# Values of six token-tile pairs in Strassen form in the key/value stage of a linear-attention and SwiGLU kernel, with the x sums for the FFN kept on chip

## The chip, the cores and the metric

The kernel runs on one core of a Trainium2 chip. The metric is the device time of one execution in microseconds (us). A time of the whole kernel is the median of several runs; the trace and the profile come from one execution that was recorded. The engines are named as the profile names them: PE (matrix products; PEld is its weight loading), DVE (vector engine), ACT (scalar engine), POOL (GpSimd) and SP (which issues most DMA transfers). Each runs its own instructions in the order in which they were laid down, and waits on the others by semaphores.

## The reference, cut to what matters

S = 2048 tokens, D = 576, 32 heads of 18, F = 4608, all float32.

```python
qkv = split_heads(x @ wqkv)
pq, pk = q @ w_phi, k @ w_phi                       # per head
phi_q = concat(softmax(pq), softmax(-pq))
phi_k = concat(softmax(pk), softmax(-pk))
kv = einsum("bhsf,bhsd->bhfd", phi_k, v)            # summed over the tokens
z = einsum("bhsf->bhf", phi_k)
o = (phi_q @ kv) / (phi_q . z + 1e-6)
s = merge_heads(o) @ wo

xn = layernorm(x);  attention runs on xn
g = silu((silu(xn @ w_gate) * (xn @ w_up)) @ w_down)
return x + s * g
```

## The kernel before

**Number format.** A float32 value is held as two parts that PE multiplies at its faster float32r rate: a rounded high part (H, hi) and the rest, the low part (L, lo). A product x·w is hi·hi + hi·lo + lo·hi. D = 576 is cut into two halves of 288 (HALF), and each half of the contraction into two full chunks of 128 rows and a tail of 32 rows; for the tail the high and low parts lie on different partitions of one tile, so that a single matmul of 96 rows does all three products. So `xw` (L82) takes 14 matmuls for a 288-column product of a token tile: 2 halves of the contraction, with 3 + 3 + 1 each.

**Stages.** (1) Preparation, to 70.8 us: layernorm of the token blocks, transposes, and splitting of x into `X` (list `XB`) and of the weights into `KVWH`/`KVWL` (K weights folded with w_phi, then V weights). (2) The key/value stage, 70.8 to 227.6 us: 16 token tiles of 128. For each, K in two halves (28 matmuls into the PSUM tile `p2`, of which there is one buffer), its softmaxes (`softmax_parts`, L268 to L282: on DVE maximum, subtraction, minimum, subtraction, on ACT two exponentials, on DVE sum and reciprocal, then the product of L356 that gives `phi`), V in two halves (14 matmuls each into a tile `p`, copied by ACT to `v`, L364 to L369), and `kv_step` (L286: ten float32 products of phi with v, 20 records, accumulated over all tiles in the three PSUM tiles `kvp`). The `kv_step` of a tile is issued in the middle of the next one. (3) A transition: the column of ones in v has given z, which ten small copies bring to `zc`; matmuls with `ident` spread it over the partitions (L391), ACT copies it to `zb` (L394); the kv blocks are masked to `km` (L398) and split to KVH and KVL. (4) The Q stage (to about 470 us): Q projections, softmaxes, and attention output. (5) The FFN, already in Strassen form, to the end.

**Work beside the stages.** Some FFN tiles are computed early, in plain form, by `early_tile` (14 matmuls of 512 columns into PSUM tiles `pe`, silu on ACT, product on DVE). A scheduler lays the instructions out on the engines, and pe matmuls go where the main order leaves PE free. `spread_out` (L325) makes the x sums that the Strassen FFN reads: for each of eight token stacks k a load of the float32 tail of x into `sraw` (`load_stack`), additions of hi and lo (`raw_x`), four sums (`sums`), and `sum_parts`, which casts the sums to `shi` on ACT (L319), subtracts the tails on DVE (L320) and the rest on POOL (L321), and stores both to `sum_dram`. It has two `sraw` buffers and is stepped four times for each token tile. Stack k has two token tiles of one sequence half, four tiles apart; with the two halves of the contraction these make the four x blocks of a stack, a 2 by 2 blocking of x.

**Memory.** The tiles of these stages come from pools on two sides of SBUF; a new tile waits until earlier users of its place are done.

## Time and profile before

| | us |
|---|---|
| three runs | 1646.59, 1646.65, 1647.71 |
| median | 1646.65 |
| the execution that was profiled | 1646.79 |
| its span | 1645.0 |
| PE busy in the span | 1611.2 |
| preparation | 0 to 70.8 |
| key/value stage | 70.8 to 227.6 |
| transition | 227.6 to 238.2 |
| Q stage | 238.2 to about 470 |
| FFN | about 470 to 1645 |

How to read the rows that follow. A row of the timeline has the start in us, the duration, the engine, the line of the kernel, the operation, the tile written and the tiles read, the shape, and how many such instructions it groups (x20); in brackets stands the idle time of the engine just before it and what ended that idle time. A matmul's shape is rows of the contraction * columns of the stationary operand, then the output's columns. A row of the groups (by line, engine and shape) has busy us and the mean ns of one, then idle time before it by what ended it. A row of DMA issues has the transfer, the queue, the count, the size and the median us from issue to landing.

### The profile page before, as it was taken

To read this page: it belongs to the slowest core of one execution; us is meant where nothing else is said; L and a number is where in the kernel's file an instruction comes from. 1 tells how busy PE (TensorE), PEld (TensorE's weight loads), DVE (VectorE), ACT (ScalarE), POOL (GpSimd) and SP (SyncE) were. 2 spreads that over 40 slices of the span, in tenths; PEclk is the share of its full clock that TensorE was granted. 3 is DMA by queue.
4 is the path that set the end of the run, shared out by engine and by line. 5 is a ranking of instruction groups with operands and counts; after the bars stand their busy time and mean duration, and the time that the engine had idled before them with its cause. 6 is when DMAs were issued, how large, how long until landed. Compare 5 with 4: busy or idle time off the path is not lost.

```text
span 1645.0 us, 25213 instructions
## 1 busy us (share of the span) xinstructions
PE 1611.2 (98%) x9441; PEld 1435.0 (87%) x9441; DVE 1177.0 (72%) x1722; ACT 715.3 (43%) x1389; POOL 619.4 (38%) x660
## 2 busy tenths in 40 slices
PE   6999999999999999999999999999999999999998
PEld 5899998999987788888888888888888888888887
DVE  7678759899852476887887778845566677666578
ACT  5533345444431365444444444445433333333334
POOL 3466500343202353653554454412333244133132
PEclk9999999999999999999999999999999999999999
DMA  9623313343218545555455545495545556555434
GB/s 290 212 78 109 110 34 112 92 143 110 74 45 293 202 169 180 173 175 177 175 172 171 183 166 176 130 364 164 164 127 161 170 173 211 161 179 183 140 114 173
DMA packets 118108, 264.69 MB, mean 161 GB/s; under 512 B 12418, under 2 KB 48386, under 8 KB 116194
## 3 DMA queue, kind: packets, MB, share of 16 engines
q1 hardware_dynamic: 107628, 247.44, 45.7%
q0 software_dynamic: 3072, 11.02, 2.4%
q10 hardware_dynamic: 7286, 4.63, 0.9%
q8 instruction: 74, 1.21, 0.3%
q14 instruction: 48, 0.39, 0.1%
HBM read 164.21 MB, written 98.83 MB: 160 GB/s over the span
## 4 chain that ended last, share of the span: by engine, by line
PE 66%; DVE 1%; DMA 0%; issue 0%; ACT 0%; POOL 0%; SPq 0%; ACTq 0%; POOLq 0%; DVEq 0%
PE pd L669 24%; PE px L570 23%; PE pw L570 11%; PE py L570 6%; PE pe L92 2%; DVE acc L641 0%; DMA hb<-h_dram 0%; DVE w L59 0%; DMA X<-s_dram 0%; DVE hh L59 0%; ACT w L58 0%; DVE acc L642 0%; ACT s L599 0%; POOL ld L560 0%; DVE s L604 0%
## 5 line engine op out<-in xcount | busy, mean ns | idle before, releaser
L669 PEld LDWEIGHTS pd<-dw,hh 128*128 128x128 f32 x3048 | 431.8, 188 | 23.0 <-ACT pd L690 1.5
L669 PE MATMUL pd<-dw,hh 128*128 128x288 f32 x3048 | 447.4, 297 | 1.7 <-ACT pd L690 0.7
L570 PE MATMUL px<-X,w 128*128 128x512 f32 x1440 | 373.2, 393 | 4.6 <-ACT s L599 3.6
L570 PEld LDWEIGHTS px<-X,w 128*128 128x128 f32 x1440 | 261.3, 188 | 55.9 <-ACT s L599 6.9
L570 PE MATMUL pw<-X,w 128*128 128x512 f32 x720 | 185.5, 393 | 0.0
L570 PEld LDWEIGHTS pw<-X,w 128*128 128x128 f32 x720 | 134.8, 189 | 30.1
L92 PE MATMUL pe<-X,wh 128*128 128x512 f32 (+1 forms) x480 | 152.0, 400 | 1.9 <-DVE h L120 0.9
L604 DVE TENSOR_TENSOR s<-pw,s 128x512 f32<-128x512 f32 x120 | 82.5, 688 | 99.1 <-ACT s L599 88.3
L794 DVE TENSOR_TENSOR acc<-pd,acc 128x576 f32<-128x576 f32 x128 | 96.2, 752 | 79.4 <-PE pd L669 79.3
L599 ACT COPY s<-px 128x512 f32<-128x512 f32 x120 | 70.4, 586 | 154.7 <-PE px L570 154.7
L58 ACT CAST hh<-ha 128x512 fp32r<-128x512 f32 x140 | 82.7, 619 | 96.2 <-PE pd L669 71.0
L92 PE MATMUL p<-KVWH,X 128*128 128x288 f32 (+1 forms) x640 | 123.6, 298 | 0.7 <-DVE phi L274 0.7
L59 DVE TENSOR_TENSOR hh<-ha,hh 128x512 fp32r<-128x512 f32 x140 | 110.6, 815 | 17.6 <-ACT hh L58 15.9
L766 POOL TENSOR_TENSOR hb<-hb 128x512 f32<-128x512 f32 x34 | 45.8, 1346 | 163.8 <-DVE hb L626 163.3
L92 PEld LDWEIGHTS pe<-X,wh 128*128 128x128 f32 (+1 forms) x480 | 88.5, 189 | 19.9 <-DVE h L120 1.7
L92 PEld LDWEIGHTS p<-KVWH,X 128*128 128x128 f32 (+1 forms) x640 | 100.5, 188 | 1.4 <-issue 1.1
L59 DVE TENSOR_TENSOR w<-ld,w 128x512 fp32r<-128x512 f32 (+1 forms) x90 | 76.6, 852 | 33.2 <-ACT w L58 32.1
L570 PE MATMUL px<-X,wt 96*128 96x512 f32 x240 | 94.8, 395 | 0.0
L570 PE MATMUL py<-X,w 128*128 128x512 f32 x360 | 93.7, 395 | 0.1
L779 POOL TENSOR_TENSOR ha<-ha 128x512 f32<-128x512 f32 x34 | 52.6, 1562 | 107.2 <-DVE hh L59 107.2
L58 ACT CAST w<-ld 128x512 fp32r<-128x512 f32 (+1 forms) x90 | 49.4, 549 | 86.6 <-POOL ld L560 54.3
L753 POOL TENSOR_TENSOR h<-ha,hb 128x512 f32<-128x512 f32 x34 | 44.9, 1320 | 103.3 <-DVE ha L630 66.6
(181 smaller groups left out, 3046.5 us busy)
## 6 DMA issues: line engine op xcount, KB each, us to landing
w_dram<-w SPq DMA_DIRECT2D x87, 512.0 KB, 2.8
w<-w_dram SPq DMA_DIRECT2D x87, 512.0 KB, 4.4
wt<-t_dram SPq DMA_DIRECT2D x59, 336.0 KB, 3.4
ld<-in_B_w_gu SPq DMA_DIRECT2D x30, 512.0 KB, 4.5
X<-sum_dram SPq DMA_DIRECT2D x8, 1280.0 KB, 7.0
rt<-in_B_w_down SPq DMA_DIRECT2D x33, 288.0 KB, 3.4
rb<-in_B_w_down SPq DMA_DIRECT2D x33, 288.0 KB, 4.5
w_dram<-w SPq DMA_DIRECT2D x29, 256.0 KB
```

What stands on the lines that cost most here:

```text
L58: nc.scalar.copy(hi, src)
L59: nc.vector.tensor_sub(lo, src, hi)
L92: nc.tensor.matmul(ps, l, r, start=n == 0, stop=n == len(pairs) - 1)
L570: nc.tensor.matmul(ps, l, r, start=first and n == 0, stop=last and n == len(mm) - 1, skip_group_check=True)
L599: nc.scalar.copy(t, ps)
L604: nc.vector.tensor_add(t, ps, t)
L669: nc.tensor.matmul(ps, l, r, start=first and n == 0 and m == 0, stop=n == len(hs) - 1 and m == 2, skip_group_check=True)
L753: sub(s, g["h"][0][0], g["h"][0][1])
L766: nc.gpsimd.tensor_add(a21, a21, g["h"][1][1])
L779: sub(a12, a12, g["h"][0][0])
L794: nc.vector.tensor_add(a2, pd[:, :, 0:HALF], a2)
```

## The change

Pairs p = 2 to 7 of token tiles (stack k = (p + 4) mod 8; a pair is the two token tiles of a stack that share its weights) compute their values as a 2 by 2 by 2 Strassen product: seven products of 288 by 288 instead of eight. Four of its x operands are the blocks of x, the other four are the x sums of the FFN, which `sum_parts` now leaves in `shi` and `slo` on chip (and still stores). Three of its weight operands are new sums, `TH`/`TL`, made by `v_sums` while the first tiles run; `v_first` rewrites the second V half of the first contraction half in KVWH and KVWL to a difference. Products shared by two outputs are added by DVE (`v_add`), and one is copied from bank `vx` to `vy` to go on accumulating there. Pairs 0 and 1 stay plain. The x sums follow the order 6, 7, 0, 1, ..., one stack ahead of its use, through one `sraw` buffer; the tail subtraction goes from DVE to POOL; the last stack's sums come after the last pair. The first token half of the early FFN tiles 0 and 1 that is computed (i = 1) is now issued whole before the stage, and the PSUM pool `eps` is closed there; a new one, `eps2`, opens after the stage. `m` has one buffer instead of two, and the pool `qc` opens after the stage.

```diff
@@ preparation's end, pools
+                for f in range(2):
+                    early_tile(f, 1, first_weights[f])
-            qc = att.enter_context(tc.tile_pool(name="qc", bufs=1, side="right"))
...
-            kk = kst.enter_context(tc.tile_pool(name="kk", bufs=2))
-            kps = kst.enter_context(tc.tile_pool(name="kps", bufs=1, space=PSUM))
+            pes.close()
+            kt = wst.enter_context(tc.tile_pool(name="kt", bufs=1, reuse_waits="tile"))
+            TH = kt.tile([P, 3, 3, HALF], F32R, name="TH")
+            TL = kt.tile([P, 3, 2, HALF], F32R, name="TL")
+            kk = kst.enter_context(tc.tile_pool(name="kk", bufs=2, side="right", reuse_waits="tile"))
+            kvs = kst.enter_context(tc.tile_pool(name="kvs", bufs=1, space=PSUM, reuse_waits="tile"))
+            kps = kst.enter_context(tc.tile_pool(name="kps", bufs=1, space=PSUM, reuse_waits="tile"))
...
-                m = kk_pool.tile([P, 2, H], F32, name="m")
+                m = kk_pool.tile([P, 2, H], F32, name="m", bufs=1)
...
-                raws[k] = kk.tile([P, 4, 3, P], F32, name="sraw", bufs=2)
+                raws[k] = kk.tile([P, 4, 3, P], F32, name="sraw", bufs=1)
...
+            def sum_parts(k):
+                r = raws[k]
+                lo = los[k] = kk.tile([P, 4, 2, P], F32R, name="slo", bufs=1)
+                for a in (2, 0):
+                    j = slice(a, a + 2)
+                    hi = his[k, a] = kk.tile([P, 2, 3, P], F32R, name="shi", bufs=2)
+                    tc.keep_in_program_order(nc.scalar.copy(hi, r[:, j]))
+                    nc.gpsimd.tensor_sub(hi[32:64, :, 2], r[32:64, j, 2], hi[32:64, :, 2])
+                    nc.gpsimd.tensor_sub(lo[:, j], r[:, j, 0:2], hi[:, :, 0:2])
+                    nc.sync.dma_start(sum_dram[k // 4, :, j, k % 4, 0:3], hi.bitcast(F32))
+                    nc.sync.dma_start(sum_dram[k // 4, :, j, k % 4, 3:5], lo[:, j].bitcast(F32))
...
-            def sum_parts(k, a):
...
-                tc.keep_in_program_order(nc.vector.tensor_sub(hi[32:64, :, 2], r[32:64, j, 2], hi[32:64, :, 2]))
-                nc.gpsimd.tensor_sub(r[:, j, 0:2], r[:, j, 0:2], hi[:, :, 0:2])
...
+            def v_sums(c):
+                t = kk.tile([P, 4, 3, P], F32, name="sraw", bufs=1).rearrange("p a b n -> p (a b n)")
...
+                for k, m in ((0, 0), (1, 2)):
+                    nc.sync.dma_start(t[:, m:m + 2], w_v[:, k, c].rearrange("p (a n) -> p a n", a=2))
+                sub(t[:, 2], t[:, 2], t[:, 0])
+                sub(t1[:, c] if c < 2 else t1t, t[:, 0], t[:, 1])
+                add(t[:, 1], t[:, 1], t[:, 2])
+                sub(t[:, 3], t[:, 3], t[:, 1])
+                nc.scalar.copy(TH[:, :, c], t[:, 1:4])
+                if c < 2:
+                    nc.vector.tensor_sub(TL[:, :, c], t[:, 1:4], TH[:, :, c])
                 else:
+                    nc.gpsimd.tensor_sub(TH[64:96, :, 2], t[64:96, 1:4], TH[64:96, :, 2])
+
+            def v_first():
+                hi, lo = KVWH[:, 0, :, V2], KVWL[:, 0, :, V2]
+                nc.scalar.copy(hi[:, 0:2], t1)
+                nc.scalar.copy(hi[:, 2], t1t)
+                nc.vector.tensor_sub(lo, t1, hi[:, 0:2])
+                nc.gpsimd.tensor_sub(hi[64:96, 2], t1t[64:96], hi[64:96, 2])
...
+            def v_product(ps, x, w, first, last):
+                wh, wl = vws[w]
+                mm = [m for c in range(2) for m in ((x[c], wh[:, c]), (x[c], wl[:, c]), (x[3 + c], wh[:, c]))]
+                mm += [(x[2][0:96], wh[0:96, 2])]
...
+            def v_add(v, ps):
+                with tc.high_priority():
+                    for d, src in v_parts(v, ps, 0):
+                        nc.vector.tensor_add(d, src, d)
...
+                        if p == 0 and j == 0:
+                            for c in range(3):
+                                v_sums(c)
+                        elif p == 0:
+                            load_stack(order[0])
+                            raw_x(order[0], 0, 1)
+                            raw_x(order[0], 2, 3)
+                        elif j == 0:
+                            sums(order[0])
+                    if p == 1:
+                        v_first()
+                        sum_parts(order[0])
+                        load_stack(order[1])
+                    continue
...
+                phi0 = k_tile(ts[0])
+                vx, vy, vw = (kvs.tile([P, 512], F32, name=n) for n in ("vx", "vy", "vw"))
+                v_product(vx, x[0], 0, True, False)
+                with tc.high_priority():
+                    nc.scalar.copy(vy[:, 0:HALF], vx[:, 0:HALF])
+                raw_x(order[p - 1], 0, 1)
+                kv_step(*pend)
+                v_product(vw, x[7], 1, True, False)
+                with tc.high_priority():
+                    v_copy(v1, vw, 0)
+                v_product(vy, x[1], 2, False, True)
+                v_copy(v0, vy, 1)
+                raw_x(order[p - 1], 2, 3)
+                v_product(vx, x[4], 4, False, False)
+                with tc.high_priority():
+                    v_copy(v0, vx, 0)
+                phi1 = k_tile(ts[1])
+                sums(order[p - 1])
+                v_product(vw, x[5], 3, False, True)
+                v_add(v0, vw)
+                v_product(vx, x[6], 5, False, False)
+                v_add(v1, vx)
+                v_product(vx, x[3], 6, False, True)
+                v_copy(v1, vx, 1)
+                kv_step(2 * p, phi0, v0)
+                pend = (2 * p + 1, phi1, v1)
+                sum_parts(order[p - 1])
+                load_stack(order[p])
...
             kv_step(*pend)
+            raw_x(order[7], 0, 1)
+            raw_x(order[7], 2, 3)
+            sums(order[7])
+            sum_parts(order[7])
```

The scheduler decides how these calls stand on the engines. Three places show it. The rows name the line, the operation, the tiles (with their buffer numbers) and the shape.

ACT in the second and third tile of the stage, before: `phi` rows are the exponentials, the `v` rows the copies of V.

```order
L277 ACTIVATE phi<-phi 128x576
L364 COPY v_607<-p 128x2x126
L366 COPY v_607<-p 128x36
L277 ACTIVATE phi<-phi 128x576
L364 COPY v_607<-p 128x126
L368 COPY v_607<-p 128x90
L369 COPY v_607<-p 128x72
L277 ACTIVATE phi<-phi 128x576
```

The same place on ACT after the change, where L346 casts the weight sums to TH:

```order
L281 ACTIVATE phi<-phi 128x576
L346 CAST TH<-sraw 128x3x288
L281 ACTIVATE phi<-phi 128x576
L386 COPY v_746<-vx 128x90
L386 COPY v_746<-vx 128x126
L386 COPY v_746<-vx 128x72
L346 CAST TH<-sraw 128x3x288
L281 ACTIVATE phi<-phi 128x576
L386 COPY v_745<-vy 128x2x126
```

A cast of weight sums now stands between the exponentials of a tile.

PE at the end of a Strassen pair, after the change: L375 are the value products, L294 is `kv_step`, and the last row is the first K matmul of the next pair.

```order
L375 MATMUL vx<-TL,shi 128x288
L375 MATMUL vx<-TH,slo 128x288
L375 MATMUL vx<-TH,shi 128x288
L294 MATMUL kvp_796<-v_745,phi 72x73 x2
L294 MATMUL kvp_794<-v_745,phi 126x127 x4
L375 MATMUL vx<-TH,X_67 128x288
L375 MATMUL vx<-TL,X_67 128x288
L375 MATMUL vx<-TH,X_67 128x288 x2
L375 MATMUL vx<-TL,X_67 128x288
L375 MATMUL vx<-TH,X_67 128x288 x2
L294 MATMUL kvp_795<-v_745,phi 126x127 x4
L92 MATMUL p_1338<-KVWH,X_64 128x288
```

The `kv_step` of the pair's first tile lies in and behind its last product, and there is nothing else between it and the next K.

ACT in the transition, before: `zc` and `zb` are the copies of z, KVH the splitting of kv.

```order
L385 COPY zc<-kvp_614 72x1 x2
L58 CAST KVH<-km 126x126
L394 COPY zb<-p_2181 128x504
L58 CAST KVH<-km 126x126 x2
L116 ACT_TABLE_LOAD
L116 ACTIVATE h<-pe 128x512
L394 COPY zb<-p_2181 128x504
```

ACT in the transition, after the change, where L325 casts the last stack's x sums:

```order
L494 COPY zc<-kvp_796 72x1 x2
L58 CAST KVH<-km 126x126 x2
L503 COPY zb<-p_2351 128x504
L58 CAST KVH<-km 126x126 x3
L503 COPY zb<-p_2351 128x504
L325 CAST shi<-sraw 128x768 x2
L503 COPY zb<-p_2362 128x72
L58 CAST KVH<-km 126x126 x2
L503 COPY zb<-p_2362 128x72
```

Two casts of x sums now stand between the large and the small copies of zb.

## The prediction

> **What bounds the kernel now.** I read the engines' busy times first, then five windows cut at the stages of the program, then PE's waits, then the rows at the places that the change touches.

> ```profile
> PE 1611.2 (98%) x9441; PEld 1435.0 (87%) x9441; DVE 1177.0 (72%) x1722; ACT 715.3 (43%) x1389; POOL 619.4 (38%) x660
> 70.80:227.60 156.80, 156.14 (x1232) 155.02 (x1232) 116.28 (x136) 49.79 (x137) 86.21 (x82) 1.00 0.26 86
> 227.60:238.20 10.60, 10.60 (x68) 9.24 (x68) 4.78 (x19) 5.70 (x21) 0.00 (x0) 1.00 0.11 30
> 238.20:470.00 231.80, 228.90 (x1499) 207.44 (x1497) 205.68 (x315) 109.24 (x182) 63.76 (x128) 1.00 0.33 102
> ```

> A window's row has its length, then busy time and instructions of PE, PEld, DVE, ACT, POOL, the granted clock, the DMA share and GB/s. PE is the bound: in the key/value stage (70.8 to 227.6) it idles 0.66 of 156.8 us, in the transition after it not at all, at a granted clock of 1.00. So a matmul taken from this stage is worth its full time, if PE is not made to wait for someone else; and DVE (74% there) and POOL (55%) work close beside it.

> **Part A: fewer matmuls.** One token tile late in the stage:

> ```profile
> 200.83 2.18 PE L290 MATMUL kvp<-v,phi 128*126 128x127 f32 x20
> 202.82 0.38 PE L92 MATMUL p<-KVWH,X 128*128 128x288 f32 x1
> ...
> 210.36 2.18 PE L290 MATMUL kvp<-v,phi 128*126 128x127 f32 x20
> ```

> From 202.82 to 210.36 PE runs the 56 projection matmuls of a tile (28 for K, 28 for V): 7.54/56 = 0.135 us each. The kv_step takes 202.82 − 200.83 = 1.99, so a tile lasts 9.53 and a pair 19.06. In the six Strassen pairs the values take seven products of 7 matmuls, 49, in place of 56, of the same 288 columns; the order of PE confirms 42 fewer. 42 × 0.135 = **−5.65 us**. That is the most the change can bring, apart from B: 0.34% of the time.

> **Part B: the one wait of the stage.**

> ```profile
> 75.56 0.06 DVE L264 MEMSET v<- 128x4 f32 x1 [5.49 <-DMA x_dram<-xr]
> 78.86 0.37 PE L92 MATMUL p<-KVWH,X 128*128 128x288 f32 x1 [0.66 <-DVE phi L274]
> ```

> Before the first softmax DVE stands at the memset of v, until the transfer x_dram<-xr gives that memory free; tile 1's K then waits 0.66 us for the K bank, which DVE reads last. In the new order v lies elsewhere and its memset waits for early DVE and POOL work only. I take **−0.66**; the bounds are −0.66 and 0.

> **Part C: the start of the stage.** While the first four tiles run plainly, POOL, ACT and DVE make the weight sums TH and TL in three rounds through a single sraw buffer, then v_first, then the first x sums.

> ```profile
> rt<-in_B_w_down SPq DMA_DIRECT2D x33, 288.0 KB, 3.4
> rb<-in_B_w_down SPq DMA_DIRECT2D x33, 288.0 KB, 4.5
> sraw<-x_dram SPq DMA_DIRECT2D x8, 256.0 KB, 3.0
> 81.01 1.01 POOL L310 TENSOR_TENSOR sraw<-sraw 128x384 f32<-128x384 f32 x1
> 82.10 2.01 POOL L311 TENSOR_TENSOR sraw<-sraw 128x384 f32<-128x384 f32 x1
> 81.89 1.36 DVE L356 TENSOR_TENSOR phi<-phi,sm 128x1152 f32<-128x1152 f32 x1
> L319 ACT CAST shi<-sraw 128x768 fp32r<-128x768 f32 x16 | 13.0, 844 | 11.2 <-POOL sraw L321 7.1 <-DMA sum_dram<-shi 4.2
> ```

> A round is a chain: load 3.4 (the 288 KB row), four POOL operations of 288 columns (1.01 × 288/384 = 0.76 each, 3.1), the cast of 864 columns (0.84 × 864/768 = 0.95), the subtraction on DVE (1.36 × 864/1152 = 1.0), handoffs 0.4: 8.9 us, and only then may the next load overwrite the buffer. From the first K matmul on, the casts come at about 9.1, 18.0 and 26.75. ACT runs in order, and the new order puts each cast ahead of an exponential: tile 1's second exponential could run at about 14.5 (K ends at 11.3, DVE's four passes take 3.0) but stands behind the second cast until 18.95; then exponential 0.6, sum 1.35, reciprocal 0.55, product 1.36 end at 22.8, with handoffs 23, and PE wants that phi at 7.54 + 9.53 + 3.77 + 1.87 = 22.7. Such near misses I work out at the kv_steps of tiles 0 to 3: 0.4, 0.5, 0.25 and 0.8, the last behind the two shi casts, which stand there waiting for POOL's sums. Sum **+2.0**; with loads of 3.0 us it is 1.3, with the 4.5 us of the other 288 KB row, in all three rounds, 4.5. What queues behind these waits: on ACT the copies of V, on PE everything.

> The row at 82.10 shows POOL's same operation at 2.01 instead of 1.01, while DVE runs its product of two SBUF operands (81.89 to 83.25). [...]

> **Part D: the six pairs.** K's bank p2 is single, so the next tile's K waits until DVE's second subtraction has read it.

> ```profile
> 208.71 0.76 DVE L273 TENSOR_REDUCE m<-p 128x32 f32<-128x576 f32 x1 [2.43 <-PE p L92]
> 209.50 0.76 DVE L274 TENSOR_TENSOR phi<-p,m 128x576 f32<-128x576 f32 x1
> 210.18 0.75 DVE L273 TENSOR_REDUCE m<-p 128x32 f32<-128x576 f32 x1
> 210.96 0.76 DVE L274 TENSOR_TENSOR phi<-p,m 128x576 f32<-128x576 f32 x1
> L398 DVE TENSOR_TENSOR km<-kvp,mask 126x126 f32<-126x126 f32 x8 | 2.1, 286 | 1.8 <-ACT zc L385 1.6
> L120 DVE TENSOR_TENSOR h<-pe,h 128x512 f32<-128x512 f32 x1 | 0.7, 692 | 0.0
> ```

> Today 28 V matmuls and a kv_step, 5.8 us, cover these four passes (208.71 to 211.72, 3.0). In a pair's second half only 21 matmuls and a kv_step remain after the last K matmul (2.83 + 1.99 = 4.82), and DVE gets four additions of the values (252 and 36 columns, twice; one operand in PSUM, one in SBUF). The trace has two operations of that kind: 126 columns 0.286, 512 columns 0.692, so about 1.05 ns per column on 0.15: 0.42 and 0.19, twice, is 1.2. Lag 0.2 + passes 3.0 + additions 1.2 = 4.4 of 4.82: the cover holds with 0.4 to spare. The tail subtraction of the x sums, 0.86 each, leaves DVE for POOL.

> ```profile
> L320 DVE TENSOR_TENSOR shi<-sraw,shi 32x256 fp32r<-32x256 f32 x16 | 13.8, 864 | 2.8 <-ACT shi L319 2.4
> L321 POOL TENSOR_TENSOR sraw<-sraw,shi 128x512 f32<-128x512 f32 x16 | 22.5, 1417 | 29.6 <-ACT shi L319 29.6
> L305 POOL TENSOR_TENSOR sraw<-X 128x256 f32<-128x256 f32 x26 | 22.0, 867 | 2.9 <-DMA sum_dram<-sraw 2.5 <-DVE shi L320 0.3
> ```

> POOL's chain for one pair of x sums: two tails and two low parts (0.86 + 1.42, twice, 4.6), four raw_x (3.5, beside the load), four sums (1.0 to 1.3, 4.5), gaps 0.9: 13.5 us against a pair of 18.1. It hides with 4.6 to spare, casts and stores included. PE uses the same results from the chip one pair later, so the slack is also theirs. I take **+0.3** for D (bounds 0 and the 6.6 of the second rival).

> **Part E: the end of the stage.**

> ```profile
> 225.47 2.19 PE L290 MATMUL kvp<-v,phi 128*126 128x127 f32 x20
> 227.50 1.10 PE L391 MATMUL p<-ident,zc 126*128 126x126 f32 x8
> ...
> 229.27 1.16 PE L391 MATMUL p<-ident,zc 126*128 126x126 f32 x8
> ...
> 238.94 0.86 PE L92 MATMUL pe<-X,wh 128*128 128x512 f32 x3
> 239.64 0.40 PE L92 MATMUL pe<-X,wl 128*128 128x512 f32 x1
> ```

> The last x stack is now made after the last pair, and ACT's order puts its two shi casts between the two large copies of zb and the small ones. PE's last zc matmul waits for a small copy, so it waits for POOL. From the last K matmul of the last pair: the casts of the stack before end at 7.35; POOL's tails and low parts (0.63 and 1.27, undisturbed) bring 10.4; then the load of the last stack (it needs the single buffer) 13.8; four sums at 1.0 to 17.8; cast 18.75, copy and PE at 19.1. PE's own work until there: 4.8, then 16 pe matmuls of 0.233 (239.64 − 238.94 over three) 3.7, kv_step 2.0, zc 2.6, 14 more pe matmuls 3.3: 16.4. Stall **+2.7**; 2.0 with every POOL step at its fastest row, 4.3 with low parts at 1.42 and tails at 0.86 as well as a load of 3.4. Today nothing of the kind is behind the zb copies, and PE is fully busy there.

> **Part F: work that moves.**

> ```profile
> 51.56:70.79 19.23, 18.06 (x134) 16.50 (x133) 11.68 (x17) 15.34 (x21) 5.62 (x17) 1.00 0.59 213
> ```

> The early FFN tiles before the first K matmul are now closed off whole, 112 pe matmuls in place of 109, in a stretch where PE is already 94% busy (18.06 of 19.23); the stage itself has no pe matmuls in its gaps until its end. There are as many in all, at the same shapes, so PE's work is conserved. The Q stage, whose order changes a little, had 2.9 us of PE idle to gain or lose from (231.80 − 228.90): 0 ± 1. The FFN's order is unchanged.

> **Sum.** −5.65 − 0.66 + 2.0 + 0.3 + 2.7 + 0 = −1.3. The profiled execution took 1646.79 (span 1645.0 and 1.8 around it), 0.14 above the median of 1646.65, so the forecast is 1646.65 − 1.3 = **1645.3 us**.

> **Rivals.** *First, both ends are hidden.* If the sums at the start run at the fastest rows (1.3) and the last stack at the end is early enough, or its casts late enough, that PE loses 0.7 there, the sum is −5.65 − 0.66 + 1.3 + 0.7 = −4.3: 1642.3. For it: each miss is under 1 us and each chain has several handoffs that I estimated. Against it: the casts stand in ACT's order ahead of work that PE needs, and POOL is far from idle at both places.

> *Second, slower: K's bank becomes the clock of the pair.* If an addition costs 0.69 even at 252 and 36 columns, the four take 2.77 and DVE needs 0.2 + 3.0 + 2.8 = 6.0 after the last K matmul against 4.82 of cover: 1.1 a pair, 6.6 over six; the sum is −1.3 + 6.3 = +5.0: 1651.6. It decides from the point where the additions together exceed 1.6 us, or one of them waits on its product while a pass stands behind it. For it: only 0.4 us of spare. Against: the 126-column row is at 0.286.

> That the change doesn't do what it says is excluded by the count of matmuls in its order.

> **How the numbers follow.** Forecast (saving mostly paid back at both ends) 0.43, own range 1643.4 (C 1.3, E 2.0) to 1649.9 (C 4.5, E 4.3, F 1, cut at the bound of no change); first rival 0.34; second 0.23. A difference of 0.2% (3.3 us) is about what a measurement can tell from none. The first rival lies below that bound (1643.4), the second above (1649.9), so faster 0.34, same 0.43, slower 0.23. The range that leaves out a small part of each outer case is 1641.5 to 1651.5.

> **What would show it.** A: 42 fewer 288-column matmuls, and a pair of 18.1 us between the same kv_steps. B: the 0.7 row of PE's waits on phi gone. C: PE idle before kvp matmuls in the first four or five tiles, 2 us together, released by DVE's phi. D: no wait of a K matmul on DVE in the pairs; the additions at about 0.42 and 0.19. E: one wait of PE on the copy of zb, of 2 to 4 us, with the shi casts ahead of it waiting for POOL. The forecast is wrong if PE idles over 2 us in the six pairs, or over 1 us more than before in the Q stage, or not at all at the ends.

## The result, and the profile after

The changed kernel takes 1654.24 us (median of 6 runs, 1653.29 to 1657.84) beside 1646.81 us of the kernel before: ratio 1.0046, 95% interval 1.0036 to 1.0056, so 7.4 us slower. The forecast was 1645.3 us, in a range from 1641.5 to 1651.5.

First the windows of the kernel before, cut at five marks: PE's first transposition, its first K matmul, its first zc matmul, its first Q matmul, the first Strassen product of the FFN. So the transition ends here at the first Q matmul, 3.7 us earlier than in the windows ahead. Columns as there.

```profile
0.00:10.39 10.39, 0.00 (x0) 0.00 (x0) 5.61 (x20) 2.00 (x3) 2.18 (x9) 1.00 0.81 255
10.39:70.79 60.40, 54.39 (x325) 46.28 (x326) 46.01 (x98) 41.95 (x58) 23.18 (x43) 1.00 0.83 276
70.79:227.50 156.71, 156.05 (x1231) 154.93 (x1231) 116.28 (x135) 49.69 (x135) 86.22 (x82) 1.00 0.26 87
227.50:234.51 7.01, 7.01 (x42) 5.66 (x41) 4.22 (x18) 5.76 (x22) 0.00 (x0) 1.00 0.00 0
234.51:539.37 304.86, 301.36 (x1861) 267.53 (x1861) 224.61 (x345) 124.68 (x212) 72.82 (x139) 1.00 0.39 124
539.37:1645.00 1105.63, 1092.35 (x5989) 960.64 (x5987) 780.26 (x1108) 491.19 (x963) 434.99 (x388) 1.00 0.54 175
```

The same windows of the changed kernel:

```profile
0.00:11.48 11.48, 0.00 (x1) 0.01 (x1) 5.97 (x20) 2.00 (x3) 2.20 (x9) 1.00 0.82 256
11.48:72.55 61.07, 54.86 (x329) 46.66 (x330) 46.09 (x96) 41.04 (x57) 22.88 (x42) 1.00 0.74 249
72.55:228.08 155.53, 152.31 (x1191) 150.26 (x1190) 115.09 (x148) 56.06 (x148) 106.00 (x101) 1.00 0.29 93
228.08:240.69 12.61, 9.63 (x46) 6.79 (x45) 7.91 (x18) 5.61 (x22) 10.92 (x12) 0.89 0.38 129
240.69:545.39 304.70, 300.30 (x1850) 266.22 (x1851) 224.63 (x344) 127.31 (x214) 73.91 (x139) 1.00 0.39 126
545.39:1652.30 1106.91, 1093.80 (x5989) 961.86 (x5987) 781.35 (x1108) 491.28 (x963) 436.26 (x388) 1.00 0.53 175
```

Length less PE's busy time is PE's idle time. The counted work moves by the 42 matmuls (−5.65) and by pe matmuls of 0.233 us (3 more before the first K, 2 in the key/value stage, 4 in the transition, 9 fewer behind it). That gives, in us:

| stretch | length | counted work | PE idle | rest of busy |
|---|---|---|---|---|
| to the first transposition | +1.09 | 0 | +1.09 | 0 |
| preparation | +0.67 | +0.70 | +0.20 | −0.23 |
| key/value stage | −1.18 | −5.18 | +2.56 | +1.44 |
| transition | +5.60 | +0.93 | +2.98 | +1.69 |
| Q stage | −0.16 | −2.10 | +0.90 | +1.04 |
| FFN | +1.28 | 0 | −0.17 | +1.45 |
| sum | +7.30 | −5.65 | +7.56 | +5.39 |

So the matmuls are gone, and PE's idle time alone eats them; what was not in the sum at all is the last column. PE's waits in the changed kernel (total us, times, longest):

```profile
PE tp L191 <- DVE xn L179: 13.3, 2, 11.5
PE p L591 <- ACT so L594: 4.1, 6, 1.3
PE kvp L294 <- DVE phi L401: 3.1, 3, 1.7
PE p L500 <- ACT zb L503: 2.8, 2, 2.4
PE px L681 <- ACT s L710: 2.7, 2, 2.2
```

The kvp row is 0.67 and 1.67 at the start of the stage and 0.74 at its last kv_step; the zb row is the end. PE's timeline there, and under it a window:

```profile
236.86 0.44 PE L500 MATMUL p<-ident,zc 72*128 72x72 f32 x2 [2.41 <-ACT zb L503]
...
237.88 1.35 PE L92 MATMUL pe<-X,wh 128*128 128x512 f32 x3
...
240.69 0.58 PE L92 MATMUL p<-QH,X 128*128 128x288 f32 x1 [0.17 <-DVE km L507]
```

```profile
238.00:241.40 3.40, 3.23 (x10) 2.14 (x9) 2.55 (x8) 0.70 (x3) 2.18 (x2) 0.50 0.79 274
```

About 1 us after the wait of 2.41 us has ended, the same three matmuls that took 0.86 in the kernel before take 1.35. For 3.4 us the granted clock is 0.50, which is 1.7 us of PE's work: 1.35 of it in the transition, most of its "rest" of 1.69, and 0.35 behind it. But the low clock is not what makes the transition long. The run e5_start below ends the stage with the same instructions in the same order, has a wait of 2.50 us at the same place and keeps a clock of 1.00 (the three matmuls take 0.86 there), and its transition takes 12.68 us. Its PE:

```profile
235.03 0.44 PE L508 MATMUL p<-ident,zc 72*128 72x72 f32 x2 [2.50 <-ACT zb L511]
...
238.85 0.37 PE L92 MATMUL p<-QH,X 128*128 128x288 f32 x1 [1.24 <-DVE km L515]
```

From the row behind the wait for zb to the first Q matmul pass 3.82 us here and 3.83 in the changed kernel. In both, the first Q matmul starts about 0.15 us behind the end of DVE's last mask (km); the low clock only fills a wait that PE has in any case. DVE in the changed kernel shows what its masks and the low parts of kv (KVL) wait for:

```profile
237.03 1.29 DVE L59 TENSOR_TENSOR KVL<-km,KVH 126x126 fp32r<-126x126 f32 x2 [2.33 <-ACT KVH L58]
...
240.33 0.22 DVE L507 TENSOR_TENSOR km<-kvp,mask 72x72 f32<-72x72 f32 x1
```

The 1.45 of the FFN is of another kind again. Behind a wait of 2.2 us at 583 us the clock is at 0.50 for 3.4 us. The kernel before has that wait too, and in its profiled execution no drop. The next product of that kind, before and then changed:

```profile
581.03 1.65 PE L570 MATMUL px<-X,w 128*128 128x512 f32 x6 [0.84 <-ACT s L599]
```

```profile
587.57 1.54 PE L681 MATMUL px<-X,w 128*128 128x512 f32 x6
```

PE is busy 1.4 us longer up to there, but the wait of 0.84 us is gone by it: what follows comes 0.4 us later. Of the 1.28 us by which the FFN is longer, another 0.3 come at a wait near 1364 us, and 0.5 lie behind PE's last matmul (7.38 us to the end of the span, 6.89 before). That last part takes 7.3 to 7.9 us in all ten profiles with Strassen pairs and 6.0 to 6.9 in the four without, so it belongs to the change; no run shows why.

ACT in the transition shows whom PE waits for:

```profile
231.71 0.57 ACT L503 COPY zb<-p 128x504 f32<-128x504 f32 x1
233.69 0.83 ACT L325 CAST shi<-sraw 128x768 fp32r<-128x768 f32 x1 [1.41 <-POOL sraw L315]
235.86 0.83 ACT L325 CAST shi<-sraw 128x768 fp32r<-128x768 f32 x1 [1.33 <-POOL sraw L317]
236.59 0.21 ACT L503 COPY zb<-p 128x72 f32<-128x72 f32 x1
236.70 0.49 ACT L58 CAST KVH<-km 126x126 fp32r<-126x126 f32 x2
```

The first small copy of zb stands behind two casts, and these behind POOL's sums; the casts of KVH, for which DVE waits, stand behind them too. The pairs, by PE's timeline (the first and last rows are the mid-pair kv_step of two successive pairs):

```profile
189.44 2.27 PE L294 MATMUL kvp<-v,phi 128*126 128x127 f32 x20
...
199.99 1.42 PE L294 MATMUL kvp<-v,phi 128*72 128x73 f32 x12
201.16 0.38 PE L375 MATMUL vx<-TH,X 128*128 128x288 f32 x1
...
207.71 2.27 PE L294 MATMUL kvp<-v,phi 128*126 128x127 f32 x20
```

A pair takes 18.27 us where the count gives 18.11, with no wait in it.

### The profile page after: what moved, and what is told of

It is laid out like the page before. It is cut to its first block, busy times and chain, and to the rows that moved or that the text cites. A ratio compares the mean times of both kernels' runs of the same rounds, so it can differ in the third digit from the quotient of the medians.

```text
span 1652.3 us, 25216 instructions
## 1 busy us (share of the span) xinstructions
PE 1610.9 (97%) x9399; PEld 1431.8 (87%) x9399; DVE 1181.0 (71%) x1733; ACT 723.3 (44%) x1402; POOL 652.2 (39%) x690
## 4 chain that ended last, share of the span: by engine, by line
PE 87%; DMA 5%; DVE 3%; POOL 2%; ACT 2%; issue 1%; SPq 0%; ACTq 0%; POOLq 0%; DVEq 0%
PE pd L780 24%; PE px L681 23%; PE pw L681 11%; PE pe L92 7%; PE py L681 6%; PE p L92 5%; PE p L591 3%; PE po L577 2%; PE kvp L294 1%; PE vx L375 1%; PE pt L571 1%; DMA s_dram<-so 1%; DMA xn<-in_A_x 1%; DMA sraw<-in_A_w_v 1%; PE vw L375 1%
## 5 line engine op out<-in xcount | busy, mean ns | idle before, releaser
L92 PE MATMUL pe<-X,wh 128*128 128x512 f32 (+1 forms) x480 | 152.7, 402 | 2.7 <-ACT h L117 1.4
L92 PEld LDWEIGHTS pe<-X,wh 128*128 128x128 f32 (+1 forms) x480 | 88.7, 190 | 20.8 <-ACT h L117 1.7
L722 ACT COPY py<-px 128x512 f32<-128x512 f32 x60 | 34.3, 572 | 97.4 <-PE px L681 81.8
L92 PE MATMUL pe<-X,wl 128*128 128x512 f32 x192 | 76.9, 401 | 0.0
## 6 DMA issues: line engine op xcount, KB each, us to landing
rt<-in_B_w_down SPq DMA_DIRECT2D x33, 288.0 KB, 3.1
rb<-in_B_w_down SPq DMA_DIRECT2D x33, 288.0 KB, 4.9
w_dram<-w SPq DMA_DIRECT2D x29, 256.0 KB, 2.2
```

The source lines that it names most:

```text
L92: nc.tensor.matmul(ps, l, r, start=n == 0, stop=n == len(pairs) - 1)
```

## The experiments

Each was timed beside the kernel before on the same chip; the kernel before had medians from 1646.8 to 1648.4 us there, so the ratio is the number to compare, and marks and idle times come from one profiled execution each. PE's idle time in the Q stage is that between the first Q matmul and the first FFN product (before 3.5, changed 4.4 us).

| run | median, us | before, us | ratio, 95% interval | Q stage idle, us |
|---|---|---|---|---|
| changed kernel | 1654.24 | 1646.81 | 1.0046 (1.0036 to 1.0056) | 4.4 |
| e1_end | 1657.12 | 1647.62 | 1.0047 (1.0032 to 1.0061) | 7.3 |
| e2_so | 1652.15 | 1647.62 | 1.0032 (1.0021 to 1.0043) | 2.9 |
| e3_plain | 1656.41 | 1647.62 | 1.0051 (1.0036 to 1.0066) | 8.5 |
| e4_end_so | 1650.08 | 1647.62 | 1.0015 (1.0005 to 1.0024) | 3.6 |
| e5_start | 1653.58 | 1648.26 | 1.0030 (1.0018 to 1.0042) | 6.1 |
| e6_all | 1647.42 | 1648.26 | 0.9995 (0.9986 to 1.0004) | 4.5 |
| e7_before_so | 1647.31 | 1648.26 | 0.9995 (0.9986 to 1.0004) | 2.7 |
| e8_no_last | 1649.87 | 1648.26 | 1.0007 (0.9998 to 1.0016) | 5.0 |
| e9_tile | 1645.45 | 1648.42 | 0.9984 (0.9975 to 0.9994) | 1.7 |
| e10_tl | 1647.30 | 1648.42 | 0.9990 (0.9982 to 0.9999) | 2.2 |
| e11_plain_mended | 1648.91 | 1647.47 | 1.0007 (0.9999 to 1.0016) | 2.4 |
| e12_best_again | 1644.55 | 1647.47 | 0.9978 (0.9968 to 0.9988) | 2.3 |

**The end moved back (e1_end).**

```diff
             sums(order[7])
-            sum_parts(order[7])
...
                 split(KVH[0:w, i, 0:w], KVL[0:w, i, 0:w], km[0:w, 0:w])
+            sum_parts(order[7])
```

> The casts and low parts of the last x stack (sum_parts of order[7]) are issued behind the last zb copy and the splitting of kv; nothing else changes. Theory 1 (the end of the stage costs what its two waits show plus the low clock behind them: 0.4 + 2.4 us of waiting, and some 1.7 us of matmuls at a granted clock of 0.6 to 0.8): the waits of PE on ACT's zb copies vanish, the clock stays at 1.00 in the 5 us behind the transition, the first Q matmul starts 4 to 5 us earlier, and the time falls from 1654.2 to 1649 to 1650.5. Theory 2 (the wait only moves: the Q stage cannot begin before the memory of the x sums is free): PE waits as long at its next instruction, 1652.5 or more.

The transition takes 7.87 us instead of 12.61, at a clock of 1.00: theory 1 for the place. Of these 4.7 us, 1.2 are five pe matmuls that now stand in the Q stage; 3.6 are mended. The time doesn't follow, theory 2 for the sum. Its waits from 70 to 545 us:

```profile
PE p L591 <- ACT so L594: 5.1, 4, 2.0
PE kvp L294 <- DVE phi L401: 3.9, 4, 1.6
PE p L92 <- DVE e L278: 1.6, 1, 1.6
```

The Q stage has a wait of 2.0 us for so, with a clock of 0.50 for 3.4 us behind it, and a new one of 1.6 for the second Q softmax.

**Two buffers of so (e2_so), and with the end (e4_end_so).**

```diff
-                    so = qk.tile([P, D], F32, name="so", bufs=1)
+                    so = qk.tile([P, D], F32, name="so", bufs=2)
-                y = qk.tile([P, 2 * H], F32, name="y")
+                y = qk.tile([P, 2 * H], F32, name="y", bufs=1)
```

> The output tile so of the projection gets a second buffer (and y one instead of two, to make room); the key/value stage is as in the changed kernel. Theory 1 (the Q stage lost 2 us because the projection waits for the store of so more often, six waits of 4.1 us against two of 1.5 us before): the waits of the projection on so fall below 0.5 us and the time from 1654.2 to about 1650.5. Theory 2 (DVE sets the pace of the Q stage, 85 to 90% busy there): the waits turn up at another place of the Q stage, and the time stays above 1653.

> Both edits together: the last x stack's casts behind the zb copies, and two buffers of so. If the two losses are separate they add: 4 to 5 us and 2.5 to 4 us less than the changed kernel, 1645.5 to 1648. If the Q stage only passes the stall on, no more is gained than by the first edit alone, 1649 to 1650.5.

The projection's waits fall from 4.1 to 2.0 us, not below 0.5, and the ratio by 0.0014 (2.3 us), with intervals that overlap; the time lies between those of the two theories. With both edits the ratio falls by 0.0031 (5.1 us), clear of the noise: with so mended, the end's gain stays. The sum is below the 6.5 us at least that was expected, and 1650.08 lies in the range of the other case, which however was reckoned from a gain of e1_end that did not come.

**All pairs plain (e3_plain).** `if p < 2` becomes `if p < 8`, without v_sums and v_first; raw_x, sums and sum_parts stay, one stack a pair.

> All eight pairs are plain (no weight sums, no v_first, no value additions; 896 matmuls of 288 columns again); pools, banks, early tiles and the x sums stay as in the changed kernel. Theory 1 (Strassen gains its 5.65 us less 0.9 in the pairs; start waits 2.3, and end waits with their clock 4.5, are the price of its side work; the rest, some 3 us at the program's start and in the Q stage, comes from the new arrangement): 1649 to 1652, with no wait at the kv_steps of the first tiles. Theory 2 (the new arrangement is free, all of the loss is Strassen's): 1646 to 1647.5. Theory 3 (the arrangement costs more than Strassen gains): above 1654.

Theory 3: plain, in this arrangement, is at least as slow as Strassen. Its first kv_steps have no wait, as theory 1 has it; but its Q stage idles 8.5 us, 5.5 of them at seven waits for so and 2.9 at three for the softmax. The Q stage's text is the same in all these kernels; the scheduler's order of pe matmuls in it is not.

**ACT's order at the start (e5_start).**

```diff
+                with tc.issue_after(exps[-1].ins):
+                    nc.scalar.copy(TH[:, :, c], t[:, 1:4])
...
+                    if k == order[0]:
+                        with tc.issue_after(exps[-1].ins):
+                            nc.scalar.copy(hi, r[:, j])
...
-                            for c in range(3):
-                                v_sums(c)
+                            v_sums(0)
                         elif p == 0:
+                            v_sums(1)
+                            v_sums(2)
```

> In the changed kernel, the casts of the second and third weight sums and of the first x stack may only be issued on ACT behind the last exponential of the tile that is under way, and the second and third rounds of v_sums are written one tile later; nothing else changes. Theory 1 (PE's waits at the kv_steps of the first tiles, 0.7 to 0.8 + 0.7 + 1.6 us in the profiles so far, come from ACT's order): the waits of 0.7 and 1.6 us at the second and fourth kv_step vanish, the stretch from the first K to the first zc matmul falls from 155.5 to 156.2 us to about 153.5, and the time by 2 us where the Q stage keeps its idle time. Theory 2 (the sums themselves are late, since casts and rounds of the single buffer now come later): PE waits the same 2 us at the first Strassen products instead, and the stretch stays at 155.5 or more.

Theory 1: K to zc takes 153.19 us instead of 155.53, and only the waits at the first and the last kv_step are left (0.64 and 0.74). The Strassen products did not wait. Of the 2.3 us 1.85 are idle time and 0.5 busy time. The ratio falls by 0.0016 (2.6 us), though the Q stage idles 1.7 us more here; the intervals overlap, so the gain is read from the stage's length rather than from the time.

**The three edits together (e6_all), and so in the kernel before (e7_before_so).**

> The three edits together: casts behind the exponentials at the start, last x stack behind the zb copies, two buffers of so. Theory 1 (start, end and Q stage are separate losses): the stretch from K to zc about 153.5, from zc to the first Q matmul about 8, Q stage with no more idle time than the 3.6 us of the version with two edits; 2 us less than that version, so 1648 beside a kernel before of 1647.6 on the chip of the last runs. The gain of 5.65 us then still doesn't show, since a wait of 1.6 us in the Q stage, one of 0.6 to 0.7 in the first tile, one of 0.7 at the last and some 0.9 in the pairs remain. Theory 2 (the order of the Q stage is redrawn by each edit and gives or takes as much as the edits do): anything from 1646 to 1653, with idle time of the Q stage other than 3 to 4 us.

> The kernel before with two buffers of so, as a control for the edit of so: how much of what that edit gains belongs to the change. If only the change's order makes the projection wait, it gains nothing here (within 0.5 us of the kernel before). If the wait for the store is there in both, its two waits of 1.5 us go, and the time falls by about 1.5 us.

Together they bring the ratio from 1.0046 to 0.9995, 8.4 us. The stages follow theory 1: K to zc takes 153.57 us and the transition 8.01, so the losses of start and end are separate. The Q stage follows theory 2: it idles 4.5 us, not the 3.6 at most of theory 1. In the kernel before, two buffers of so do as much as 0.0005 and not surely that; its two waits for so do vanish, so that edit mends what both have. By the medians it is worth more in the changed one (0.0014), but the intervals do not show it.

**No last stack (e8_no_last).** The load, raw_x, sums and sum_parts of order[7] are left out, and the stores of order[6] are repeated in their place; the FFN reads wrong sums for one stack.

> The changed kernel without the last x stack: its sums are left out, and the stores of the stack before are done twice, so that the FFN reads wrong sums for one stack. Theory 1 (the end of the stage costs its waits on zb and the low clock behind them, because the sums of the last stack come after the last pair): zc to the first Q matmul falls from 12.6 us to about 8, at a clock of 1.00, and the first Q softmax no longer waits for memory as it did when the casts were only moved back; with the Q stage as it was the time is 1649 to 1650. Theory 2 (that stretch is long for another reason, the splitting of kv or the early tiles' silu): it stays above 10 us.

The transition is as short as in the kernel before and without idle time:

```profile
226.57:233.35 6.78, 6.78 (x41) 5.44 (x40) 4.37 (x19) 4.09 (x20) 0.00 (x0) 1.00 0.75 241
```

and the ratio is 0.0039 (6.4 us) lower than the changed kernel's: theory 1. The transition is 5.8 us shorter, 1.2 of it by five pe matmuls that moved on; the other 4.7 make the last stack the largest single loss.

**What the moved stack still costs (e9_tile).**

```diff
-            qk = qst.enter_context(tc.tile_pool(name="qk", bufs=2))
+            qk = qst.enter_context(tc.tile_pool(name="qk", bufs=2, reuse_waits="tile"))
```

and the same for qw.

> The version with three edits (start, end, so), and the pools of the Q stage wait tile by tile for the memory that they take over, no longer for every tile of the key/value stage. In the version before it the first Q softmax stood 5 us behind its matmuls, until the stores of the last x sums had landed, and PE waited 1.9 us for the second. Theory 1 (that wait is the memory of the late x sums, the price of moving them back): DVE's first reduction of the Q stage follows the end of the Q matmuls, the wait of 1.9 us goes, and the time is 1 to 2 us below that version, 1646 beside a kernel before of 1648. Theory 2 (the Q stage's idle time depends on the whole order, not on this wait): the wait goes, and others of the projection or the softmax take its place, 1647 to 1649.

DVE's first reduction of the Q stage in e6_all, whose Q matmuls began at 233.80:

```profile
243.36 0.76 DVE L279 TENSOR_REDUCE m<-p 128x32 f32<-128x576 f32 x1 [9.16 <-DMA ez<-in_A_wo]
```

and in e9_tile, whose Q matmuls began at 233.44:

```profile
237.45 0.76 DVE L279 TENSOR_REDUCE m<-p 128x32 f32<-128x576 f32 x1 [3.60 <-PE p L92]
```

It now follows the matmuls; the releaser that the first row names is a guess of the profile's, since the tile waited for all earlier users of the pool's memory, the late stores of x sums among them. The wait of 1.9 us is gone, Q idles 1.7 us, and the time is below the kernel before with an interval that excludes 1: theory 1. The interval of the ratio still touches that of e6_all, so the trace, not the time, shows what this edit alone did.

**DVE's order at the start (e10_tl).** The subtraction for TL is issued behind the product that gives phi.

> As the version before in this call, and in addition the subtraction for TL on DVE only behind the product of the softmax that is under way. Theory 1 (the wait at the first kv_step, 0.6 to 1.0 us, is DVE's subtraction of TL and the splits behind it that stand ahead of that product): the wait falls below 0.3 us and the stretch from K to zc to about 153.0. Theory 2 (the rounds of the weight sums come later by it, and so the first Strassen products): the wait moves there.

Theory 2: the wait at the first kv_step goes, and one of 0.83 for ACT's copy of v and one of 0.31 for POOL's slo come at 114 and 116 us; K to zc 154.50 instead of 153.03. The edit gains nothing.

**What Strassen is worth in the mended surroundings (e11_plain_mended, e12_best_again).**

> All eight pairs plain, as in the plain version before, with the edits of the end (last x stack behind the zb copies), of so (two buffers) and of the Q stage's pools (waits tile by tile). It differs from the best version by the Strassen pairs and the weight sums alone. Theory 1 (the 42 matmuls are worth 5.65 us, less 0.9 us in the pairs and 1.2 us of waits at the first and last kv_step): 3.5 us slower than the best version in the same call. Theory 2 (the gain of the best version over the kernel before comes from the edits, not from Strassen): equal to it or faster.

> The best version once more (three edits and the Q stage's pools waiting tile by tile), on the chip of the plain version of this call, for the comparison with it, and for whether its gain over the kernel before (ratio 0.9984, interval 0.9975 to 0.9994) holds on another chip: expected 0.998 to 0.999.

The plain version is 4.4 us slower (1648.91, 1647.70 to 1650.55, beside 1644.55, 1642.47 to 1648.25): theory 1, since the pairs bring what was counted, as soon as nobody waits for their side work. The profiles agree: the key/value stage takes 153.19 us with 16 pe matmuls and in the plain version 154.04 with 5, so without the pe matmuls 3.4 us less, for 3.5 expected. The best version, e9_tile, repeated its gain on a second chip: 0.9978. In its profile the transition takes 7.94 us and the Q stage 303.35, with 2.3 us of idle time.

## Why the prediction was wrong, step by step

**A and B held.** 42 matmuls fewer in 9399 records against 9441, and no wait of a K matmul on phi.

**C held.** The casts to TH came 9.6, 18.4 and 26.8 us behind the first K matmul (forecast 9.1, 18.0, 26.75). The waits were 0.67 and 1.67, 2.3 in all for a forecast 2.0; two of the four forecast ones were not there, and the one behind the shi casts was twice its size:

```profile
109.07 0.83 ACT L325 CAST shi<-sraw 128x768 fp32r<-128x768 f32 x1 [1.31 <-POOL sraw L315]
111.26 0.83 ACT L325 CAST shi<-sraw 128x768 fp32r<-128x768 f32 x1 [1.35 <-POOL sraw L317]
112.00 0.68 ACT L281 ACTIVATE phi<-phi 128x576 f32<-128x576 f32 x1
```

This exponential's input was ready at 108.8. e5_start puts these casts behind it, and the wait of 1.67 us is gone: ACT's order was the cause. The wait of 0.67 goes when the subtraction for TL is moved on DVE (e10_tl), though others come for it: there DVE's order counted, which C had only as a part of its rounds.

**D held but for its small change.** K's bank never became the clock; the additions cost 0.41 and 0.18 us (forecast 0.42 and 0.19). The term was 0.3; 6 × 0.16 = 0.9 was measured: the mid-pair kv_step takes 2.07 instead of 1.99 to the next matmul, and the split of the other makes a third change back to 288-column products a pair, at some 0.08 each (0.22 after it instead of 0.13). That is read from the trace; no run took it apart.

**E is the first of two steps that failed.** Its first part was right: the casts stand in ACT's order ahead of the small copies, and PE waits 0.40 + 2.41 us for zb, for a forecast 2.7. But E ended its path at the last zc matmul and let 14 pe matmuls and the Q stage follow freely. ACT's casts of KVH stand behind the same two casts, DVE's low parts and masks of kv behind these, and the first Q matmul behind the last mask. Where the clock stays at 1.00, in e5_start, that is another wait of 1.24 us; in the changed kernel the same time goes into matmuls at the low clock and a wait of 0.17. Beside POOL's work for the last stack, DVE's last two pairs of 126-column KVL subtractions take 1.29 (at 237.03) and 1.51 us (at 238.89); such a pair at 230.78, with POOL idle, takes 0.49, and in e8_no_last, without that work, the last two take 0.50 and 0.43. POOL's tails, put at 0.63 us, have no row at that figure: the fastest in the changed kernel takes 0.72, the fastest low part the 1.27 that was put. In all the transition grew by 4.7 us beyond its four more pe matmuls, for a term of 2.7, and e8_no_last takes 4.7 away.

The last kv_step, just ahead, waited 0.74 more, which no term had. DVE's and POOL's rows show why it did:

```profile
213.28 1.36 DVE L401 TENSOR_TENSOR phi<-phi,sm 128x1152 f32<-128x1152 f32 x1
...
223.75 2.16 DVE L401 TENSOR_TENSOR phi<-phi,sm 128x1152 f32<-128x1152 f32 x1
```

```profile
213.37 2.14 POOL L314 TENSOR_TENSOR sraw<-sraw 128x384 f32<-128x384 f32 x1 [0.87 <-DMA sraw<-x_dram]
215.59 1.00 POOL L315 TENSOR_TENSOR sraw<-sraw 128x384 f32<-128x384 f32 x1
...
223.41 1.29 POOL L327 TENSOR_TENSOR slo<-sraw,shi 128x512 fp32r<-128x512 f32 x1
224.77 1.72 POOL L326 TENSOR_TENSOR shi<-sraw,shi 32x256 fp32r<-32x256 f32 x1
```

Where the two engines work on two SBUF operands at once, in these rows the one that starts later pays: POOL at 213.37 (2.14 instead of 1.00), DVE at 223.75 (2.16 instead of 1.36), then POOL at 224.77 (1.72 beside 0.73 for the same operation at 222.59). Beside DVE's subtraction from a PSUM tile at 217.38 (0.76, its usual time) POOL's row at 217.76 takes its usual 1.01. DVE's 0.8 us delay PE's last kv_step: in all ten profiles with pairs that product takes 2.15 or 2.16 us and PE waits 0.74 or 0.75, and in the two plain versions of the new arrangement it takes 1.36 and PE waits 0.22 or 0.23. The prediction's row at 82.10 (2.01 instead of 1.01) has it on POOL alone; these rows have it in both directions.

**F is the second: it put at zero what was not.** The Q stage gave +0.90 idle and +1.04 of busy time that the count does not explain; 0.35 of the latter is the end of the low clock, and no run took the rest apart. "Work conserved" was right and not enough: the order of that stage is laid out anew with every edit ahead of it, and its idle time ranged from 1.7 to 8.5 us over the runs. The FFN, whose order of matmuls is unchanged, still gave +1.28: 0.4 by the drop of the clock that the kernel before did not have in its profiled execution, 0.3 at one wait and 0.5 behind PE's last matmul. The stretch to the first transposition gave +1.09; that reads as chance, since the same instructions there took 10.4 to 11.3 us in the other 13 profiles. With the drop of the clock in the FFN some 1.5 us of the profiled 7.3 are chance. The medians differ by 7.4 too; where the other executions lost as much, their times alone do not tell.

Where the saving went, then: 42 matmuls −5.65; waits in the key/value stage +2.6 and other busy time there +0.5, of which e5_start removes 2.3 by the start's order; pairs +0.9; the last stack +4.7, removed by e8_no_last; Q stage +1.9; FFN +1.3; start +1.1. Together that is the 7.3, or 8.6 more than the forecast −1.3: 2.7 of it by E with the last kv_step, 4.3 by F, and 1.6 by the start of the stage, the pairs and the other busy time there.

The second rival named a time of 1651.6, nearer to the result than the forecast, but that would have been luck: K's bank, its mechanism, never made PE wait. Of the signs that were to prove the forecast wrong none came: PE had no wait in the six pairs before the last kv_step but the one behind the shi casts, 0.90 us more in the Q stage, and waits at both ends. They asked for idle time alone and looked neither at the stretch behind the zb copies nor at busy time.

## What to carry to other kernels

Look for the last piece of background work: it no longer has main work beside it. When it is put into an engine's order, follow every engine's chain behind it up to the next stage, and not only the first wait that it causes. Compare lengths of stretches, and not busy time: the low clock behind the wait of 2.41 us added 1.35 us to PE's busy time in the transition and next to nothing to its length, since another wait followed that it filled (3.83 us to the first Q matmul, beside 3.82 at a clock of 1.00). When an edit early in a scheduled kernel changes the order of a later stage, compare that stage's idle time before judging the edit, and undo one loss at a time only together with a look at the waits, since e1_end mended 3.6 us at its place and showed nothing. Memory that passes from one pool to the next is a dependency: in e6_all, whose last x sums are stored late, the first reduction of the Q stage started 9.56 us behind the first Q matmul, and 4.01 us in e9_tile, where the pools wait tile by tile.

## What was not expected of the hardware

What a drop costs is less than the 1.7 us that it takes from PE's clock (3.4 us at 0.50). At the place near 580 us the work that follows comes 0.43 to 0.48 us later in the ten profiles with a drop, and at most 0.06 later in the other three than in the kernel before; in the transition it cost nothing that could be measured. How much of the spread of several microseconds between the runs of one kernel comes from it is not shown.
